# Attention and routed experts: the block of values one chunk later, the load of V in its own pair

## The chip, the cores and the metric

The kernel runs on one core of a Trainium2 chip. The metric is the device time of one execution in microseconds: the median of several runs, lower is better. Engines are called PE or TensorE (matmul; PEld is its weight load), ACT or ScalarE, DVE or VectorE, POOL or GpSimd, and SP, which here only issues DMAs.

## The reference

Attention for 8 batches of 8 heads, 576 positions, 64 features, with a decaying bias from a running sum, is followed by a layer of 8 experts of which each of the 4608 tokens takes one:

```python
scores = scale * np.matmul(q, k.transpose(0, 1, 3, 2))
cum = np.cumsum(np.maximum(s, 0.0), axis=-1)
bias = -(cum[:, :, :, None] - cum[:, :, None, :])
scores = np.where(causal, -1000000000.0, scores + np.minimum(bias, 0.0))
scores = scores - np.max(scores, axis=-1, keepdims=True)
attn = np.exp(scores)
attn = attn / (np.sum(attn, axis=-1, keepdims=True) + 1e-09)
x = np.matmul(attn, v)            # then heads side by side: 4608 x 512
...
e_idx = np.argmax(x @ w_gate + modality_bias[modality_id], axis=1)
...
h = np.maximum(x[mask] @ w1[e], 0.0)
out[mask] = gate_w[mask, None] * (h @ w2[e])
```

## The kernel before

**Two stages.** The attention stage takes some 380 us of the span, the expert stage the rest. The expert stage begins when attention's last rows have been written, gathered and turned.

**Pairs and chunks.** The 64 (batch, head) combinations are worked as 32 pairs: two batches of one head. The rows of scores of a pair are cut into nine chunks: 0 to 3 are the four blocks of 128 rows of the first batch, 4 to 7 those of the second, 8 is the last 64 rows of both together. The mask is causal, so chunk `c` or `4 + c` is 128 x 128(c + 1), and chunk 8 is 128 x 576. `ORDER = (3, 7, 2, 6, 8, 1, 5, 0, 4)` is the order in a pair, the wide ones first.

**One loop of steps.** `run` (L500) has one step for each chunk, nine a pair; `k % 9` is the step in the pair. A step does, in the order of the text:

- `score` (L375): the scores of this chunk by matmuls on PE (L372 and L394; L407 and L408 for chunk 8) into a PSUM buffer `sp` (four buffers); the bias, the mask and the row minimum of the negated scores on DVE (L396, L410); the exponential on ACT (L416).
- sometimes a piece of set-up, a load (`load_v`, L307, in step 5; `load_qk`, L300, in step 7), and a piece of `prep` (L312) for the next pair: copies to KB by DMA (L332), splitting of Q and K into high and low parts on POOL (L322, L326).
- a piece of `tail` (L455) of the pair before, if one is open.
- `trans` (L418) for the chunk of three steps ago (`LAG = 3`): transposes on PE (L433, L448) into a PSUM buffer `pt` (two buffers), copied to PT in SBUF by ACT (L437) or, for chunk 8, by DVE (L451, L453). Chunks 0 and 4, and chunks 1 and 5, share one buffer and one copy (`JOINT`): nothing is done at the first of the two. The transposes of the last chunk of a pair thus come in step 2 of the next pair, and with them the tail of the pair is opened.
- pieces of routing work (`bg`), in steps 0, 1 and 5 (`QUIET`) or in each step.

**The tail.** It is a generator, one piece a step. It first yields `TD` times, then does the block of values (L474): 36 matmuls that multiply PT by V into PSUM `o` and one buffer of `sp`, and the copies to `oT` on ACT (L477) and DVE (L480). The next piece makes the reciprocal row sums `rs` (L484, L485) and the first products of `oT` with the gate weights (L346, `pw` and `pq`, into PSUM `ox`, taken to `x` by DVE, L495 and L497), the piece behind it the second products. With `TD = 1` the block is in step 4.

**What sets the order.** A planner puts the instructions of each engine in order by a model of its own; where two are ready it goes by the text. It may move work, but not past explicit orders: the block stands behind every matmul and transpose of PE recorded since the last block (`self.pe`), and everything of attention that PE gets after it in the text stands behind the block (`wall`, through `behind`). So the block is a fence on PE. Each engine then takes its work in that order; DMAs of SP are issued one after the other.

**V.** `V` has two buffers. The first two loads are made before the loop. In step 5 of pair `pi` the load for pair `pi + 1` follows; it takes the buffer that the block of pair `pi - 1`, one step earlier, has read. `start` takes the tile out of `self.V` when the pair begins.

Of the kernel before, what the change touches and what calls it, by code (L numbers as in the profile page):

```python
# [23 lines left out]
EXT = 76  # L24
ORDER = (3, 7, 2, 6, 8, 1, 5, 0, 4)
LAG = 3
TD = 1
SPB = 4
PTDVE = (8,)
JOINT = (0, 1)  # L30
# [8 lines left out]
class Attn:  # L39
# [318 lines left out]
        return after  # L358

    def start(self, pi, x):  # L360
        st = dict(pi=pi, h=pi % 8, x=x, s={}, high={}, PT=self.PT[pi % 2], V=self.V.pop(pi))
        st["mx"] = self.sm.tile([P, 10], F32, name="mx")
        st["sums"] = self.sm.tile([P, 9], F32, name="sums")
        return st
# [90 lines left out]
    def tail(self, st):  # L455

        nc = self.nc
        V, PT, x, h = st["V"], st["PT"], st["x"], st["h"]
        for _ in range(TD):
            yield  # L460
# [39 lines left out]
    def run(self, npair, newx, done, setup):  # L500

        bg = self.bg = []
        seq = [(pi, i) for pi in range(npair) for i in ORDER]
        sts = {}
        prev, prepg, n = [], None, len(seq)
        for k in range(n + LAG + 9):
            if k < n:
                pi, i = seq[k]
                if k % 9 == 0:
                    sts[pi] = self.start(pi, newx(pi // 8) if pi % 8 == 0 else sts[pi - 1]["x"])  # L510
                    prepg = self.prep(pi + 1) if pi + 1 < npair else None
                with self.behind() if pi or not self.pe else self.tc.issue_after(self.pe[-1]):
                    self.score(sts[pi], i)
                if k in setup:
                    with self.newest():
                        more = setup[k]()
                        if more is not None:
                            bg.append([more, False])
                if k % 9 == 5 and 0 < pi < npair - 1:
                    self.V[pi + 1] = self.load_v(pi + 1)  # L520
                if k % 9 == 7 and 0 < pi < npair - 2:
                    self.raw[pi + 2] = self.load_qk(pi + 2)
                if prepg is not None:
                    next(prepg, 0)
            if prev and next(prev[0][0], 0) == 0:
                _, st = prev.pop(0)
                if st["pi"] % 8 == 7:
                    bg.append([done(st["pi"] // 8, st["x"]), False])
            for j in () if k == LAG else (0, 1) if k == LAG + 1 else (k - LAG,) if LAG < k < n + LAG else ():
                p0, i0 = seq[j]  # L530
                with self.behind():
                    self.trans(sts[p0], i0)
                if i0 == ORDER[-1]:
                    prev.append((self.tail(sts[p0]), sts[p0]))
            if not prev and k >= n + LAG:
                break
            for b in list(bg):
                if k >= b[1] if b[1] > 1 else k % 9 in QUIET or not b[1]:
                    with self.newest():
                        b[1] = next(b[0], None)  # L540
                    if b[1] is None:
                        bg.remove(b)
        assert not prev
        return bg
# [847 lines left out]
```

## Time and profile before

| | us |
|---|---|
| median of 3 runs | 834.55 |
| lowest, highest | 834.48, 834.68 |
| profiled execution: its own time | 833.09 |
| profiled execution: span of the trace | 831.3 |
| block of values, start to start, in most pairs | 10.8 to 11.4 |
| the block itself, modelled ends | 2.96 |

The span runs from the first to the last instruction of the trace; the execution's own time includes what lies around it. The granted clock of TensorE is 0.996 of full over the span and 1.00 in the attention stage after the start. A row of the timeline gives start, length, engine, line of the kernel, operation and operands, `xN` for N like ones in a row, and in brackets the idle time of the engine before it and what ended it.

### The profile page before, as it was taken

How to read it: one execution, taken by the hardware profiler on the slowest of the kernel's cores; microseconds unless marked ns; L12 is line 12 of the kernel's file. 1: busy time of each engine (PE TensorE's matmuls, PEld its weight loads, DVE VectorE, ACT ScalarE, POOL GpSimd, SP SyncE). 2: the span in 40 equal slices, each digit the busy share in tenths (PEclk: the TensorE clock that was granted, in tenths of full speed). 3: DMA queues.
4: the chain of work that ended last, by engine and by line, in shares of the span. 5: the costliest groups of instructions: out<-in, count | busy, mean ns of one | idle time of the engine just before them, and what ended most of it. 6: DMA issues, size and time to landing. Idle time of an engine off the chain costs nothing. (4 is left out here: it accounts for less than half of the span.)

```text
span 831.3 us, 17195 instructions
## 1 busy us (share of the span) xinstructions
PE 807.9 (97%) x5948; PEld 696.2 (84%) x5948; DVE 526.3 (63%) x1405; ACT 524.6 (63%) x1164; POOL 360.8 (43%) x383
## 2 busy tenths in 40 slices
PE   7999999999999999998999999999999999999996
PEld 6777778887787788877888999998888999988884
DVE  7555566655666666756479865565666655555865
ACT  6767778877887878875365554454455554444653
POOL 8768778888789877993501000000000000000002
PEclk9999999999999999999999999999999999999999
DMA  7575466676557655558597866565556776555960
GB/s 235 156 222 173 139 213 192 211 233 205 162 175 229 204 180 178 183 182 292 202 394 292 312 257 256 200 223 204 208 203 245 257 257 245 203 206 207 376 235 29
DMA packets 68551, 182.35 MB, mean 219 GB/s; under 512 B 7993, under 2 KB 8889, under 8 KB 68334
## 3 DMA queue, kind: packets, MB, share of 16 engines
q1 hardware_dynamic: 62622, 161.17, 57.7%
q0 software_dynamic: 5840, 20.06, 6.2%
q8 instruction: 48, 0.79, 0.4%
q14 instruction: 41, 0.34, 0.1%
HBM read 144.73 MB, written 26.80 MB: 206 GB/s over the span
## 5 line engine op out<-in xcount | busy, mean ns | idle before, releaser
L1073 POOL DMA_INDIRECT out<-ys,oi x36 | 37.1, 1031 | 370.2 <-ACT ys L1072 298.9
L416 ACT ACTIVATE pe<-pe,mx 128x512 f32<-128x512 f32 (+3 forms) x256 | 142.6, 559 | 12.1 <-DVE mx L396 11.5
L396 DVE CUSTOM_DVE_ANT_0 pe<-sp,mk 128x512 f32<-128x512 f32 (+3 forms) x256 | 117.8, 485 | 48.2 <-PE sp L394 22.7
L437 ACT COPY PT<-pt 128x512 f32<-128x512 f32 (+1 forms) x192 | 94.1, 505 | 41.8 <-PE pt L433 41.7
L433 PE MATMUL pt<-ident,pe 128*128 128x128 f32 x640 | 109.2, 277 | 3.6 <-ACT pe L416 2.9
L372 PE MATMUL sp<-KA,QH 128*128 128x256 f32 (+2 forms) x256 | 98.9, 393 | 3.5 <-POOL KA L236 2.5
L1089 ACT ACTIVATE hT<-hp 128x512 fp32r<-128x512 f32 x72 | 42.9, 596 | 92.8 <-PE hp L1087 92.3
L474 PE MATMUL o<-PT,V 128*64 128x256 f32 (+3 forms) x512 | 87.2, 440 | 4.4 <-ACT PT L437 4.3
L1087 PE MATMUL hp<-xT,wcb 128*128 128x256 f32 x648 | 89.6, 282 | 0.0
L1087 PE MATMUL hp<-xT,wca 128*128 128x256 f32 x624 | 87.3, 282 | 0.5 <-ACT xT L1039 0.5
L433 PEld LDWEIGHTS pt<-ident,pe 128*128 128x128 f32 x640 | 76.6, 143 | 13.3 <-ACT pe L416 8.3
L326 POOL TENSOR_TENSOR QL<-rawq,QH 64x576 fp32r<-64x576 f32 x62 | 86.7, 1415 | 0.1
L326 POOL TENSOR_TENSOR KA<-rawk,KA 64x576 fp32r<-64x576 f32 x62 | 86.6, 1414 | 0.3
L394 PE MATMUL sp<-KB,QL 76*128 76x256 f32 (+2 forms) x256 | 84.4, 337 | 0.5 <-DMA KB<-KA 0.4
L1087 PEld LDWEIGHTS hp<-xT,wcb 128*128 128x128 f32 x648 | 83.1, 188 | 0.6
L1090 DVE SCALAR_TENSOR_TENSOR hT<-hp,hT 128x512 fp32r<-128x512 f32 x72 | 49.5, 688 | 53.0 <-ACT hT L1089 52.9
L1087 PEld LDWEIGHTS hp<-xT,wca 128*128 128x128 f32 x624 | 80.5, 188 | 1.4 <-issue 0.7
L1062 PE MATMUL y<-wcb,hT 128*128 128x512 f32 x336 | 81.2, 398 | 0.0
L1062 PEld LDWEIGHTS y<-wcb,hT 128*128 128x128 f32 x336 | 62.8, 188 | 14.7
L474 PEld LDWEIGHTS sp<-PT,V 128*64 128x64 f32 x640 | 39.4, 137 | 34.4 <-issue 22.0
L322 POOL TENSOR_SCALAR KA<-rawk 128x576 fp32r<-128x576 f32 x60 | 39.8, 672 | 58.8 <-PE sp L372 35.3
L1087 PE MATMUL hp<-xT,wcc 128*128 128x256 f32 x456 | 64.6, 281 | 0.0
(287 smaller groups left out, 1679.6 us busy)
## 6 DMA issues: line engine op xcount, KB each, us to landing
wrbw<-in_w SPq DMA_DIRECT2D x104, 512.0 KB
wraw<-in_w SPq DMA_DIRECT2D x56, 512.0 KB
rawq<-in_qkv SPq DMA_DIRECT2D x31, 576.0 KB
rawk<-in_qkv SPq DMA_DIRECT2D x31, 576.0 KB
xg<-lists SPq DMA_DIRECT2D x18, 576.0 KB
V<-in_qkv SPq DMA_DIRECT2D x32, 320.0 KB
KB<-KA SPq DMA_DIRECT2D x62, 144.0 KB
lists<-z SPq DMA_DIRECT2D x8, 576.0 KB
```

Source lines behind the costliest of these rows:

```text
L326: self.last = nc.gpsimd.tensor_tensor(o, i, h, ALU.subtract).ins
L372: self.pe.append(self.nc.tensor.matmul(sp[:, :nn], QH[:, q0:q0 + P], self.KA[u][:, ab, :nn], start=True, stop=False).ins)
L394: self.pe.append(nc.tensor.matmul(sp[:, :nn], QL[:EXT, q0:q0 + P], KB[:EXT, ab, :nn], start=False, stop=True).ins)
L396: ins = nc.vector.tensor_tensor_reduce(out=t[:, :n], in0=sp[:, :n], in1=self.mk[:, 512 - n:512], scale=-0.125, scalar=3.0e38, op0=ALU.add, ...
L416: self.act = nc.scalar.activation(t[:, :n], t[:, :n], AF.Exp, bias=m, scale=-1.0, accum_out=st["sums"][:, o:o + 1]).ins
L433: self.pe.append(nc.tensor.transpose(out=pt[:, o:o + P], in_=pe[:, P * j:P * j + P], identity=self.ident).ins)
L437: cp(w[:, :, :, v:v + P], pt[:, :n * (1 + both)].rearrange("p (a j q) -> p a j q", a=1 + both, q=P))
L474: m = nc.tensor.matmul(t[r, q0 - b:q1 - b], V[:, ab, j, :], PT[:, ab, PTS * j + q0 if j < 4 else PTW - 64:PTS * j + q1 if j < 4 else PTW], ...
L1062: self.last[0] = nc.tensor.matmul(y[u], hT[:, a, f, P * u:P * u + P], W[4 + f // 2][:, c, 512 * (f % 2):512 * (f % 2) + 512], start=f == 0 ...
L1087: nc.tensor.matmul(hp[:, u], W[k][:, a, f:f + P], xT[:, c, k], start=k == 0 and i == 0, stop=k == 3 and i == 2)
L1089: hi = nc.scalar.activation(hs, hp, AF.Relu)
L1090: lo = nc.vector.scalar_tensor_tensor(hT[:, 1, 2 * m:2 * m + 2], hp, 0.0, hs.bitcast(F32), ALU.max, ALU.subtract)
```

## The change

`TD` becomes 2, so the tail of a pair waits one more step before the block of values: it stands in step 5 instead of step 4, and all the pieces of the tail behind it are one step later too. Since the block of pair `pi - 1` is now in step 5 of pair `pi`, after the place of the old load in the text, the load is moved: the load of pair `pi`'s own V is issued in step 2 of pair `pi`, for all pairs from 2 on. `start` accepts that V is not there yet.

```diff
-TD = 1
+TD = 2
...
-        st = dict(pi=pi, h=pi % 8, x=x, s={}, high={}, PT=self.PT[pi % 2], V=self.V.pop(pi))
+        st = dict(pi=pi, h=pi % 8, x=x, s={}, high={}, PT=self.PT[pi % 2], V=self.V.pop(pi, None))
...
-                if k % 9 == 5 and 0 < pi < npair - 1:
-                    self.V[pi + 1] = self.load_v(pi + 1)
+                if k % 9 == 2 and pi > 1:
+                    sts[pi]["V"] = self.load_v(pi)
```

## The prediction, made before the changed kernel was run

> **What bounds the kernel now.** I read the page first, then a table of windows cut from one block of values (L474) to the next, then the list of waits, then the timeline around two blocks.
>
> ```profile
> span 831.3 us, 17195 instructions
> PE 807.9 (97%) x5948; PEld 696.2 (84%) x5948; DVE 526.3 (63%) x1405; ACT 524.6 (63%) x1164; POOL 360.8 (43%) x383
> ```
>
> TensorE has no room: 97% of the span is matmul. What can be gained lies in its gaps. In the table of windows each row is one pair of the attention stage, from the start of its block to the start of the next (length, then busy time of each engine):
>
> ```profile
> 176.76:188.12 11.36, 11.04 (x95) 9.08 (x95) 6.76 (x29) 8.75 (x27) 9.46 (x11) 1.00 0.68 218
> ...
> 211.12:221.92 10.80, 10.80 (x97) 9.08 (x96) 7.00 (x32) 8.80 (x28) 7.28 (x8) 1.00 0.59 174
> ...
> 233.11:243.92 10.81, 10.81 (x97) 9.08 (x96) 7.24 (x32) 9.18 (x28) 7.75 (x9) 1.00 0.59 173
> ```
>
> The same work takes 11.36 us in one pair and 10.80 in another, at the same granted clock of 1.00: 0.56 us of the long one is no work. PE's busy time shows only 11.36 - 11.04 = 0.32 of it. The list of waits has the rest; its columns are total us, times, longest:
>
> ```profile
> PEld o L474 <- ACT PT L437: 8.0, 15, 0.7
> PEld pt L433 <- ACT pe L416: 7.7, 22, 1.3
> ```
>
> Fifteen blocks wait 8.0 us together, 0.53 us each, for a copy of PT on ScalarE, which is nearly what a long pair has over a short one. The second row, transposes that wait for an exponential, I leave as it is: the change keeps the distance from a score to its transposes.
>
> [...] The same list has this wait once more, as the matmuls show it:
>
> ```profile
> PE o L474 <- ACT PT L437: 4.3, 14, 0.5
> ```
>
> By the matmuls' row the full stake would be 4.3 us, by the loads' row 8.0. [...]
>
> Why the copy is late is seen in the timeline before the block at 188.12 (start, length, engine, line):
>
> ```profile
> 184.76 0.59 ACT L437 COPY PT<-pt 128x512 f32<-128x512 f32 x1 [1.23 <-PE pt L433]
> ...
> 185.69 0.73 ACT L416 ACTIVATE pe<-pe,mx 128x512 f32<-128x512 f32 x1
> ...
> 186.41 0.71 ACT L416 ACTIVATE pe<-pe,mx 128x512 f32<-128x512 f32 x1
> ...
> 187.12 0.60 ACT L416 ACTIVATE pe<-pe,mx 128x384 f32<-128x384 f32 x1
> ...
> 187.51 0.29 PE L408 MATMUL sp<-KB,QL 76*128 76x288 f32 x1
> ...
> 187.72 0.35 ACT L437 COPY PT<-pt 128x256 f32<-128x256 f32 x1
> ...
> 188.12 0.20 PEld L474 LDWEIGHTS o<-PT,V 128*64 128x64 f32 x4 [0.55 <-ACT PT L437]
> ```
>
> ScalarE does the three widest exponentials of the next pair (chunks 3, 7, 2) before the small copy of 256 columns that completes PT. It ends at 188.07; TensorE's scores of chunk 8 began their last matmul at 187.51 and nothing else was allowed before the block.
>
> **The change part by part.** *TD from 1 to 2.* The transposes of chunk 7 (step 4) and the score of chunk 1 (step 5) now come ahead of the block; they used to be the first thing behind it. The timeline of TensorE after the block that ends at 202.4 prices them by start to start:
>
> ```profile
> 202.36 0.66 PE L433 MATMUL pt<-ident,pe 128*128 128x128 f32 x4
> 202.77 0.36 PE L372 MATMUL sp<-KA,QH 128*128 128x256 f32 x1
> ...
> 203.09 0.66 PE L346 MATMUL ox<-pw,oT 128*128 128x144 f32 x4
> ...
> 203.76 0.49 PE L433 MATMUL pt<-ident,pe 128*128 128x128 f32 x3
> 204.00 0.36 PE L372 MATMUL sp<-KA,QH 128*128 128x256 f32 x1
> ...
> 204.33 0.49 PE L433 MATMUL pt<-ident,pe 128*128 128x128 f32 x3
> ...
> 205.87 0.40 PE L372 MATMUL sp<-KA,QH 128*128 128x512 f32 x1
> ...
> 206.34 0.65 PE L346 MATMUL ox<-pw,oT 128*128 128x144 f32 x4
> ```
>
> Transposes of 7: 202.77 - 202.36 = 0.41. Score of 1: 203.09 - 202.77 = 0.32. Together 0.73 us of work for a wait of 0.53, so at first sight all of it is covered. But PSUM's `pt` has two buffers taken in turn (chunks 3, 7, 2, 6, 8, the joint 1 and 5, the joint 0 and 4: seven a pair, so 7 takes the one that the joint 0 and 4 held). The transposes of 7 therefore cannot start before the very copy that the block waited for. Only the score of 1 covers, if the planner puts it first: 0.32 of 0.53. Ends: nothing gained (transposes first, same wait under another name), 8.0 us gained. I take the score's cover: **15 x 0.32 = 4.8 us**.
>
> *What is late next.* Behind the block the first products with the gate weights (L346) need oT, which is copied out when the block ends. The same stretch on the other engines:
>
> ```profile
> 202.30 0.59 ACT L477 COPY oT<-o 128x512 f32<-128x512 f32 x1 [1.03 <-PE o L474]
> ...
> 202.48 0.46 DVE L480 COPY oT<-sp 64x64 f32<-64x64 f32 x2 [2.76 <-PE sp L474]
> ...
> 202.98 0.55 PEld L346 LDWEIGHTS ox<-pw,oT 128*128 128x128 f32 x4
> ```
>
> oT is complete at 202.94 and its first weight load starts at 202.98: just in time. The cover was 0.73 us (7 and 1); in the new order it is the three transposes of chunk 2 (204.00 - 203.76 = 0.24) and the score of chunk 5 (204.33 - 204.00 = 0.33), 0.57 us. The load could then start 0.16 earlier, at 202.82, and would wait 0.12 us. Over 31 pairs that is 3.7 us if TensorE keeps this order, and nothing if the transposes of 6 go first. The planner does move what is not ready: the second group of these products (206.34 above) belongs to the step of chunk 5's score by the text and runs behind the next pair's first score (205.87). So I take the middle, **1.9 us lost**.
>
> *The queue of ScalarE.* The copy of oT now has the copy of 7 and the exponential of 1 ahead of it. By form, over the attention stage (count, busy us, mean ns, idle us before):
>
> ```profile
> L416 ACT ACTIVATION_READ_ACCUMULATOR pe<-pe,mx 128x1 f32 x245 | 46.3, 189 | 0.0
> ...
> L416 ACT ACTIVATE pe<-pe,mx 128x256 f32<-128x256 f32 x62 | 31.7, 511 | 5.8 <-DVE mx L396 5.8
> ...
> L477 ACT COPY oT<-o 128x512 f32<-128x512 f32 x32 | 18.8, 586 | 29.0 <-PE o L474 29.0
> ```
>
> The copy of 7 takes 0.59 (as at 184.76) and the exponential 0.51 with some 0.09 of its readout behind it: 1.19 us more. ScalarE idles 29.0 / 32 = 0.91 us before the copy of oT, and the block ends 0.73 later, so 1.64 us are there: 0.45 to spare. Cost nothing in the mean; below it is a rival, since the idle time differs from pair to pair.
>
> *The load of V.* It is issued by SP in step 2 of its own pair, not in step 5 of the pair before. SP around it, then what the page says of sizes and of the load on the queues:
>
> ```profile
> 195.83 0.47 SPq L332 DMA_DIRECT2D KB<-KA  x1
> 200.65 0.36 SPq L304 DMA_DIRECT2D rawq<-in_qkv  x1
> 203.38 0.36 SPq L304 DMA_DIRECT2D rawk<-in_qkv  x1
> 203.83 0.38 SPq L309 DMA_DIRECT2D V<-in_qkv  x1
> ```
>
> ```profile
> DMA packets 68551, 182.35 MB, mean 219 GB/s; under 512 B 7993, under 2 KB 8889, under 8 KB 68334
> ...
> rawq<-in_qkv SPq DMA_DIRECT2D x31, 576.0 KB
> ...
> V<-in_qkv SPq DMA_DIRECT2D x32, 320.0 KB
> ```
>
> Before, V left at 203.83 for the block at 221.92, 18 us ahead; its buffer was in use until 202.4, so it could not leave sooner. Now its buffer has been free since the block before, and the load follows the copies to KB into a stretch in which SP issues nothing (196.30 to 200.65). A load that leaves at 196.3 serves the block at 211.12, which will stand at about 211.9: 15 us ahead. Its 320 KB are 1.5 us at the page's mean of 219 GB/s, and with two pieces of 576 KB before it 6.7 us (an estimate from these rows). It is late only if loading takes twice that; the price would be a wait at the block, where the list has none on a DMA. Behind it on SP stand rawq and rawk, which it delays by its issue, 0.38 us, and by its 1.5 us of traffic; rawk no longer has V between it and the next copies to KB. Nothing is gained by that, since SP's idle stretch of 4.3 us lies in between. I take nothing either way.
>
> *The rest.* `start` only allows a missing V. The routing of a group begins one step later and meets the same steps 0, 1 and 5 for most of its pieces: nothing. The expert stage starts on attention's last output, so the gain carries over:
>
> ```profile
> 384.07 6.30 PE L1087 MATMUL hp<-xT,wca 128*128 128x256 f32 x48 [0.45 <-ACT xT L1039]
> ```
>
> **Sum.** -4.8 + 1.9 = -2.9 us. The profiled execution took 833.09 us (1.8 outside its span), which gives 830.2; the median of the runs shown is 834.55, 1.46 above it, which gives **831.6 us**.
>
> **The rivals.**
>
> *A, the whole wait goes.* The exponentials of 3, 7 and 2 begin earlier, because less of ScalarE's work lies between the block's end and them (copy of 7 and exponential of 1 are done), and the copy is early as in the pair of 10.80. For it: that pair exists, with the same work. Against: in the long pair ScalarE waits 1.23 us at 184.76 for TensorE, so its load there was not the limit. 834.55 - 8.0 = 826.6.
>
> *B, the wait only changes its name.* The transposes of 7 go first and wait for the same copy through `pt`; then the score, then the block. For it: that is the order of the text. Against: the planner puts ready work first. Gain 0, less up to 1.9: 834.5 to 836.5, say 835.
>
> *C, slower: the copy of oT is late on ScalarE.* The rows before 188.12 show ScalarE taking its work one piece after the other, the small copy behind three large exponentials. Where the idle time before that copy is short, the 1.19 us do not fit. One pair as it stands:
>
> ```profile
> 358.29 0.59 ACT L477 COPY oT<-o 128x512 f32<-128x512 f32 x1 [0.28 <-PE o L474]
> ```
>
> Here 0.28 + 0.73 - 1.19 = -0.18: the copy, and the products behind it, would be 0.18 us late. It is worse where the exponentials run closer together, which is what a shorter pair does. At 0.30 us late in each of 31 pairs the loss is 9.3, less the 4.8 gained: 834.55 + 4.5 = 839.0. From 4.8 / 31 = 0.15 us late per pair on, the change loses. Against it: the mean has 0.45 to spare.
>
> [...]
>
> *D, nothing of it shows:* the block keeps its place. The order behind all earlier scores and transposes is written out, so I give it little: 834.5.
>
> **How the numbers follow.** Forecast 38% (829.7 to 833.5, the two middle terms at their ends), A 20%, B 20%, C 20%, D 2%. Some 0.2%, 1.7 us, is about what a measurement can tell from no change, so faster means under 832.9 and slower over 836.2. Of the forecast three quarters are faster: 28 + 20 = 48, say 49%. Same: 10 + 15 of B + 2, 27%. Slower: C and the rest of B, 24%. The range reaches from A with another microsecond of waits gone (825.5) to C (839.0).
>
> **What would show it.** Right: the wait of `o L474` on PT falls from 8.0 us to near 0, a wait of `pt L433` on ACT PT of some 3 us appears, long pairs come to about 11.1 us. A: the long pairs are 10.8. B: that new wait is near 8 us. C: a wait of `ox L346` on ACT oT of 5 us or more, and pairs that were 10.8 are longer. It would be wrong altogether if the planner, given the new order, moves other work of the pair: the exponentials' place against the small copy decides between 10.8 and 11.36 now, and no row shows how it will fall.

## The result and the profile after

| | before | after |
|---|---|---|
| median, us | 834.51 (4 runs, 834.41 to 834.68) | 840.11 (4 runs, 838.37 to 840.92) |
| ratio after / before | | 1.0064, 95% interval 1.0047 to 1.0081 |
| span of the profiled execution | 831.3 | 838.1 |
| start of the 2nd block of values | 38.66 | 42.85 |
| start of the 32nd (last) block | 376.90 | 384.69 |
| first matmul of the experts (L1087) | 384.07 | 391.87 |

The changed kernel is 5.6 us slower, where 2.9 us faster was forecast, and it lies above C's 839.0, the upper end of the forecast's range. The table says where: 4.2 us are lost before the second block, 3.6 more up to the last block, and the expert stage of this execution is 1 us shorter (from its first matmul to the end 447.2 us before, 446.2 after). So there are two losses, in two places. Two single executions in the experiments below, one of e9 (2017 us) and one of e10 (1313 us), took far longer than the others of their kernel and are left out of the ratios, though not of the medians. The page after has TensorE as full as before:

```profile
span 838.1 us, 17128 instructions
...
PE 813.7 (97%) x5948; PEld 696.9 (83%) x5948; DVE 531.6 (63%) x1405; ACT 527.3 (63%) x1164; POOL 360.6 (43%) x383
```

97% again, though 6.8 us are lost: PE's busy time rose by 5.8 us for the same 5948 matmuls. The share of busy time does not show this loss.

**The first loss, at the start.** The table of windows cut from block to block (length, busy time of each engine with its instructions, granted clock, DMA share, GB/s), first pair before:

```profile
27.25:38.66 11.41, 11.07 (x97) 9.04 (x96) 7.90 (x38) 9.15 (x30) 6.67 (x19) 1.00 0.70 226
```

The same of the kernel after: the first pair, then a long and a short pair of the middle of the stage:

```profile
27.89:42.85 14.96, 12.92 (x96) 10.46 (x96) 8.44 (x37) 8.58 (x28) 12.04 (x29) 0.89 0.64 189
193.78:205.25 11.47, 11.12 (x96) 9.01 (x96) 6.84 (x28) 8.90 (x27) 9.06 (x10) 1.00 0.66 212
239.52:250.53 11.01, 10.99 (x96) 8.99 (x95) 6.99 (x33) 8.94 (x30) 7.77 (x9) 1.00 0.58 169
```

The first pair takes 14.96 us instead of 11.41, and POOL has 29 instructions in it, not 19. The timeline behind the first block after says what they are (start, length, engine, line):

```profile
31.90 0.23 ACT L609 CAST tok<-ti 128x36 f32<-128x36 int32 x1 [2.34 <-POOL ti L608]
...
32.11 0.20 ACT L612 CAST e<-ei 128x8 f32<-128x8 int32 x1
32.21 0.58 ACT L477 COPY oT<-o 128x512 f32<-128x512 f32 x1
32.34 1.15 DVE L614 TENSOR_SCALAR ecap<-e 128x8 f32<-128x8 f32 x1 [3.96 <-ACT e L612]
...
32.93 0.73 PE L346 MATMUL ox<-pw,oT 128*128 128x144 f32 x4 [1.38 <-ACT oT L477]
...
33.47 0.45 DVE L480 COPY oT<-sp 64x64 f32<-64x64 f32 x2
```

L609, L612 and L614 are the routing's constants: lists of numbers that POOL writes (L606, L608, L611) and ScalarE and VectorE convert, once in a run. They are made in step 5 of pair 1, where the block of pair 0 now stands. By the text they come right ahead of it, so ScalarE waits 2.34 us for POOL, VectorE 3.96 us for ScalarE, and the copies of oT stand behind both. TensorE idles 1.38 us, and the next pair starts late.

The clock has a part in it. The 0.89 of this window is one stretch of 3.41 us, from 34.37 to 37.78, at a granted clock of 0.50. Of the 3.55 us that the first pair is longer, 1.85 are longer matmuls (12.92 against 11.07 busy), and half of 3.41, some 1.7 us, is an estimate of what the low clock cost; the rest is idle time. The kernel before has such a stretch too, but at 11.69 to 15.10, ahead of its first block. In e9 below, which has the same collision, it comes at 34.78 to 38.19, again right behind the idle time. That the idle time brings it about is not shown: no run changes one without the other.

**The second loss, in every pair.** From the 4th block to the 31st are 27 pairs: before from 64.06 to 367.44, 11.236 us each; after from 68.06 to 375.58, 11.390 each. That is 0.154 a pair, 4.2 us. The long pairs went from 11.36 to 11.47, the short ones from 10.80 to 11.01. The waits of the weight loads in the attention stage after (total us, times, longest) against those quoted in the prediction:

```profile
PEld ox L346 <- DVE xq L497: 9.7, 31, 0.9
PEld pt L433 <- ACT PT L437: 7.9, 14, 0.7
PEld pt L433 <- ACT pe L416: 7.6, 21, 1.3
...
PEld o L474 <- ACT PT L437: 0.7, 1, 0.7
```

The block's wait for PT fell from 8.0 us to 0.7, and the same 8 us stand one line up, as transposes that wait for the same copy. The row on top is new but for one time of 0.9 us: the second products with the gate weights wait for VectorE in each pair. A wait that each pair had before, chunk 8's transposes for ScalarE's copies (`PEld pt L448 <- ACT PT L437`, 5.3 us, 31 times), is not in the list after. The end of a long pair after shows the first of the two:

```profile
203.78 0.29 PE L408 MATMUL sp<-KB,QL 76*128 76x288 f32 x1
...
204.02 0.28 PE L394 MATMUL sp<-KB,QL 76*128 76x256 f32 x1
...
204.26 0.35 ACT L437 COPY PT<-pt 128x256 f32<-128x256 f32 x1
...
204.66 0.66 PE L433 MATMUL pt<-ident,pe 128*128 128x128 f32 x4 [0.35 <-ACT PT L437]
...
205.25 0.65 PE L474 MATMUL o<-PT,V 128*64 128x512 f32 x2
```

The planner did put the score of chunk 1 (204.02) ahead of the transposes of chunk 7 (204.66), as the prediction had it. Yet the copy of 256 columns ends at 204.61, 0.83 us after the last matmul of chunk 8's scores began (203.78). In the pair of the prediction it was 188.07 - 187.51 = 0.56. The copy came 0.27 us later, nearly all of the 0.32 that the score covers, and the transposes wait for it in the block's stead. It is so in the other long pairs too (0.54 to 0.56 before, 0.82 or more after); why the copy is later stays open.

The second products after, with VectorE's last read of `ox`, their weight loads and their neighbours on PE:

```profile
199.73 0.28 DVE L497 TENSOR_SCALAR xq<-ox,rs 128x72 f32<-128x72 f32 x1
199.85 0.27 PE L433 MATMUL pt<-ident,pe 128*128 128x128 f32 x1
...
200.07 0.54 PEld L346 LDWEIGHTS ox<-pw,oT 128*128 128x128 f32 x4 [0.31 <-DVE xq L497]
200.07 0.76 PE L346 MATMUL ox<-pw,oT 128*128 128x144 f32 x4
...
200.66 0.49 PE L433 MATMUL pt<-ident,pe 128*128 128x128 f32 x3
...
200.91 0.48 PE L372 MATMUL sp<-KA,QH 128*128 128x512 f32 x1
```

They stand inside a group of four transposes and take 200.66 - 200.07 = 0.59 us from start to start. Before, the pair in the prediction has them between a score and transposes, at 206.34; what follows there starts 0.49 later:

```profile
206.11 0.67 PEld L346 LDWEIGHTS ox<-pw,oT 128*128 128x128 f32 x4
...
206.83 0.38 PE L433 MATMUL pt<-ident,pe 128*128 128x128 f32 x2
```

Two things differ: the neighbours, and the first weight load. Before, the load starts 0.23 us ahead of its matmul. After, it starts with it, because VectorE empties `ox` only at 199.73 + 0.28 = 200.01. The same rows over the 27 pairs, in four kernels, tell the two apart (mean us from the start of the products to the start of what follows):

| what follows | load starts ahead of its matmul | load starts with its matmul |
|---|---|---|
| transposes | 0.49 (before, 21 pairs) | 0.59 (after, 27 pairs) |
| a score | 0.40 (e11, 27 pairs) | 0.50 (e5, 16 pairs) |

A late load adds 0.10 in both rows. What stands ahead made no difference here: the products are inside transposes in 3 pairs before and in 26 after, and those 3 take 0.49 like the rest. The 0.09 between the rows of the table is not saved: a score of 512 columns took 0.32 to 0.33 us to its second matmul behind transposes or products, and 0.23 behind another score (medians, before and e11). The late load also holds its own matmul back: from the transpose ahead of it 0.21 after, 0.11 in the 3 pairs before. So **the wait for VectorE costs 0.09 + 0.10 = 0.20 us a pair** (0.198 before rounding), 5.3 us in the 27.

The first products went from 0.667 to 0.724, 1.5 us. It is the same thing in small: their first load starts 0.05 us behind the end of ScalarE's copy of oT in every pair, and 0.05 ahead of its matmul, where it was 0.12 before. No list of waits has it, since the load before it runs until then. Together 6.8 us, which is more than the 4.2 of the second loss: the pairs' other time got shorter, by 2.6.

### The profile page after: what moved, and what is told of

Same layout as the page of the kernel before. It is cut to its first block, busy times and chain, and to the rows that moved or that the text cites. A ratio compares the mean times of both kernels' runs of the same rounds, so it can differ in the third digit from the quotient of the medians.

```text
span 838.1 us, 17128 instructions
## 1 busy us (share of the span) xinstructions
PE 813.7 (97%) x5948; PEld 696.9 (83%) x5948; DVE 531.6 (63%) x1405; ACT 527.3 (63%) x1164; POOL 360.6 (43%) x383
## 5 line engine op out<-in xcount | busy, mean ns | idle before, releaser
L396 DVE CUSTOM_DVE_ANT_0 pe<-sp,mk 128x512 f32<-128x512 f32 (+3 forms) x256 | 117.7, 487 | 51.6 <-PE sp L394 28.4
L437 ACT COPY PT<-pt 128x512 f32<-128x512 f32 (+1 forms) x192 | 96.2, 502 | 48.2 <-PE pt L433 46.4
L433 PE MATMUL pt<-ident,pe 128*128 128x128 f32 x640 | 115.6, 280 | 9.0 <-ACT PT L437 5.6
L372 PE MATMUL sp<-KA,QH 128*128 128x256 f32 (+2 forms) x256 | 96.8, 385 | 2.1 <-POOL KA L236 1.8
L433 PEld LDWEIGHTS pt<-ident,pe 128*128 128x128 f32 x640 | 74.8, 143 | 24.4 <-ACT PT L437 8.9
L1087 PE MATMUL hp<-xT,wcb 128*128 128x256 f32 x648 | 89.6, 282 | 0.0
L1087 PE MATMUL hp<-xT,wca 128*128 128x256 f32 x624 | 87.3, 282 | 0.5 <-ACT xT L1039 0.4
L326 POOL TENSOR_TENSOR QL<-rawq,QH 64x576 fp32r<-64x576 f32 x62 | 87.2, 1422 | 0.1
L326 POOL TENSOR_TENSOR KA<-rawk,KA 64x576 fp32r<-64x576 f32 x62 | 86.7, 1414 | 0.2
L1087 PEld LDWEIGHTS hp<-xT,wcb 128*128 128x128 f32 x648 | 83.1, 188 | 0.6
L394 PE MATMUL sp<-KB,QL 76*128 76x256 f32 (+2 forms) x256 | 82.5, 329 | 0.4 <-DMA QL<-ek 0.4
L1087 PEld LDWEIGHTS hp<-xT,wca 128*128 128x128 f32 x624 | 80.5, 188 | 1.4 <-issue 0.7
L480 DVE COPY oT<-sp 64x64 f32<-64x64 f32 x64 | 14.2, 222 | 79.5 <-PE sp L474 79.1
```

Of the source, the lines that this page charges most:

```text
L326: self.last = nc.gpsimd.tensor_tensor(o, i, h, ALU.subtract).ins
L372: self.pe.append(self.nc.tensor.matmul(sp[:, :nn], QH[:, q0:q0 + P], self.KA[u][:, ab, :nn], start=True, stop=False).ins)
L394: self.pe.append(nc.tensor.matmul(sp[:, :nn], QL[:EXT, q0:q0 + P], KB[:EXT, ab, :nn], start=False, stop=True).ins)
L396: ins = nc.vector.tensor_tensor_reduce(out=t[:, :n], in0=sp[:, :n], in1=self.mk[:, 512 - n:512], scale=-0.125, scalar=3.0e38, op0=ALU.add, ...
L433: self.pe.append(nc.tensor.transpose(out=pt[:, o:o + P], in_=pe[:, P * j:P * j + P], identity=self.ident).ins)
L437: cp(w[:, :, :, v:v + P], pt[:, :n * (1 + both)].rearrange("p (a j q) -> p a j q", a=1 + both, q=P))
```

## The experiments

Ratios are to the kernel before, run on the same chip, with 95% intervals; "mean pair" is that of the 27 pairs, as above.

| | median us | ratio | span | mean pair |
|---|---|---|---|---|
| after | 840.11 | 1.0064 (1.0047 to 1.0081) | 838.1 | 11.390 |
| e1: after, constants in step 6 | 836.28 | 1.0042 (1.0026 to 1.0059) | 834.4 | 11.390 |
| e2: before, constants in step 4 | 835.38 | 1.0029 (1.0013 to 1.0044) | 833.1 | 11.321 |
| e3: before, load of V moved | 832.94 | 1.0001 (0.9982 to 1.0021) | 831.5 | 11.263 |
| e4: e1, row sums early | 828.83 | 0.9951 (0.9934 to 0.9968) | 827.0 | 11.121 |
| e5: before, row sums early | 828.91 | 0.9941 (0.9923 to 0.9959) | 828.0 | 11.096 |
| e6: before, joint copy on VectorE | 828.82 | 0.9938 (0.9920 to 0.9957) | 828.8 | 11.063 |
| e7: e4 and joint copy on VectorE | 827.14 | 0.9918 (0.9897 to 0.9939) | 825.3 | 10.980 |
| e8: e5 and joint copy on VectorE | 825.66 | 0.9902 (0.9871 to 0.9934) | 824.1 | 10.894 |
| e9: after, row sums early | 830.46 | 0.9946 (0.9928 to 0.9964) | 830.4 | 11.129 |
| e10: e1 and joint copy on VectorE | 830.54 | 0.9960 (0.9945 to 0.9975) | 828.0 | 11.104 |
| e11: e4, second products a step later | 817.02 | 0.9787 (0.9771 to 0.9803) | 815.9 | 10.752 |
| e12: e11 and joint copy on VectorE | 817.62 | 0.9803 (0.9786 to 0.9819) | 815.8 | 10.734 |
| e13: e5, second products in step 8 | 822.33 | 0.9861 (0.9833 to 0.9889) | 818.8 | 10.847 |
| e14: e5, second products in step 7 | 826.24 | 0.9895 (0.9876 to 0.9915) | 826.1 | 10.964 |

The kernel before had medians of 832.96 beside e1 to e4, 833.68 beside e5 to e7, 834.00 beside e8 to e10, 834.35 beside e11 and e12 and 834.45 beside e13 and e14, so medians of different groups are compared by their ratios. A single pair can differ by almost 1 us between two executions (the 30th takes 11.98 us before and 12.84 in e3), so 0.03 in the mean pair tells nothing.

**The start: e1 and e2.** e1 moves the constants behind the block; e2 gives the kernel before the same collision, since its block is in step 4.

```diff
 # e1, in the kernel after
-            setup = {..., 14: R.consts, ...}
+            setup = {..., 15: R.consts, ...}
 # e2, in the kernel before
-            setup = {..., 14: R.consts, ...}
+            setup = {..., 13: R.consts, ...}
```

> The changed kernel with the set-up of the routing constants one step later (step index 15, not 14). Theory 1: at 14 these constants stand, in the text, just ahead of the first block of values, and the copies of its result to oT queue behind them on ScalarE and VectorE; the second block then starts 4.2 us later than in the kernel before. Moved, that loss goes: 840.1 - 4.2 = 835.9, within 0.8, and the wait of 1.4 us of ox L346 on ACT oT is gone. Rival, the load of V disturbs SP's queue: no change, 840. Rival, the copy of oT is late in every pair: no change, 840.

Measured: the second block at 39.04 instead of 42.85, 3.8 us earlier, and the span 3.7 shorter; the pairs are as in the kernel after, 11.390. The window of the first pair and the timeline behind the first block in e1:

```profile
28.33:39.04 10.71, 10.71 (x97) 9.06 (x96) 6.81 (x35) 8.34 (x26) 9.53 (x27) 1.00 0.60 201
```

```profile
31.11 0.59 ACT L477 COPY oT<-o 128x512 f32<-128x512 f32 x1 [1.09 <-PE o L474]
...
33.13 0.21 ACT L609 CAST tok<-ti 128x36 f32<-128x36 int32 x1
```

The copy of oT (31.11) now runs ahead of the conversions (33.13), and the clock of this pair is 1.00, with 27 instructions of POOL in it. By the same estimate some 1.7 of the 3.8 us are the low clock, of which e1's trace has nothing in the attention stage. By the medians, each against its own kernel before, the loss went from 5.6 to 3.3 us, near what the second loss leaves; by the ratios it fell by 1.8 us only, and the intervals overlap, so the size stands on the trace.

> The kernel before with the same constants one step earlier (13, not 14), so that they stand just ahead of its own first block. Theory 1: the same collision in the kernel without the change, 834.5 + 3 to 4.5 = 837.5 to 839. Both rivals: the constants have nothing to do with it, 834.5.

Measured: the first pair takes 12.89 us instead of 11.41, 1.5 more, and the ratio gives 2.4 us. The 32nd block starts 2.2 us later (379.14 against 376.90), but that holds single pairs that differ by up to 1 us either way (the third 12.32 against 13.35, the 30th 13.07 against 11.98). The timeline of e2 has the same picture as the kernel after:

```profile
30.07 0.23 ACT L609 CAST tok<-ti 128x36 f32<-128x36 int32 x1 [1.34 <-POOL ti L608]
...
30.38 0.58 ACT L477 COPY oT<-o 128x512 f32<-128x512 f32 x1
...
31.10 0.48 PE L346 MATMUL ox<-pw,oT 128*128 128x144 f32 x2 [0.56 <-ACT oT L477]
```

The direction is right, the size smaller than expected: POOL is done sooner here, ScalarE waits 1.34 us and not 2.34, TensorE 0.56 and not 1.38, and the clock of this pair is 1.00. What follows: the first loss is this collision, with the low clock that came with it in the kernel after, and it can be had without the block's later place.

**The load of V: e3.**

```diff
 # in the kernel before, TD = 1
-                if k % 9 == 5 and 0 < pi < npair - 1:
-                    self.V[pi + 1] = self.load_v(pi + 1)
+                if k % 9 == 2 and pi > 1:
+                    sts[pi]["V"] = self.load_v(pi)
```

> The kernel before with the load of V alone moved as in the change; the block stays one step after the tail is opened. Theory 1: the load does not matter, 834.5 within 0.7. Rival, the load of V disturbs SP's queue: most of the loss is here, 838 to 840.

Measured: ratio 1.0001, and its interval leaves no room for a cost above 1.8 us. As expected against its own kernel before, the move costs nothing that is seen. (e3 has the changed `start` too.) In the kernel after SP has the load still behind rawk and as soon as the block has freed the buffer (the block ends at 208.21):

```profile
208.27 0.36 SPq L304 DMA_DIRECT2D rawk<-in_qkv  x1
208.72 0.38 SPq L309 DMA_DIRECT2D V<-in_qkv  x1
```

**The row sums: e4, e5, e9.** The reciprocal row sums `rs` are made in the block's step, not one step later. They need only the sums of the exponentials, which are there by then. It was meant to free VectorE sooner, since the second products wait for the first ones' buffer, which VectorE empties with `rs`.

```diff
             nc.vector.tensor_copy(oT[r, 512 + 64 * ab:576 + 64 * ab], ox[r, :64])
-        yield
         rs = self.sm.tile([P, 9], F32, name="rs")
         with self.tc.issue_after(self.hold[0]), self.tc.issue_after(self.act):
             nc.scalar.activation(rs, st["sums"], AF.Identity, bias=self.eps[:, :1])
             nc.vector.reciprocal(rs, rs)
+        yield
```

> The changed kernel with the constants later (as in the first run) and with the reciprocal row sums made in the step of the block, no longer one step behind it. Theory 1: the second loss is that the second products with the gate weights wait for VectorE to empty ox (L497), 9.7 us by the weight loads, 0.31 us in each of 31 pairs, because the reciprocals come late. Made early, that wait falls below 2 us and the time to 835.9 less 31 x 0.15 to 0.25, 828 to 831.5; pairs that took 11.0 to 11.1 us are back at 10.8. If that wait costs nothing, because TensorE would have waited for something else: 835.5 to 836.5. Rival, the copy of oT late on ScalarE: 836 or more, with waits of ox L346 on ACT oT.

> The kernel before with the reciprocal row sums made in the step of the block. Theory 1 (they cost only where they are late: in the kernel before, the second products do not wait for ox in steady state): no change against the kernel before, within 1.0 us, long pairs still 11.3 to 11.4. Rival (the early reciprocals are a gain by themselves, and the block one step later brought nothing to the 4.1 us by which the corrected version beat the kernel before): 4 us faster, long pairs 11.1.

e4 came out in the expected time, with the long pairs at 11.13; the short ones are 10.91, not 10.8. e5 fell against the theory on record: it expected no change and the kernel before gains as much, 0.9941. So the early sums are a gain of their own, with the block in either place. VectorE is done with `ox` (end of L497) 5.04 us behind the start of the block in e4 and 6.21 in e1, 5.15 in e5 and 6.51 before, in the mean of the 27 pairs. One row of VectorE's waits before looks like the cause and is not:

```profile
DVE pe L396 <- ACT rs L484: 22.0, 24, 0.9
```

In each of these 24 waits the row of scores gets its own matmuls only after 0.8 us, and ScalarE's part of `rs` comes 0.11 us behind them: 2.7 of the 22.0 us. Where the rest of e5's gain lies stays open, since the second products do not come late in the kernel before.

The waits of the weight loads in e4:

```profile
PEld pt L433 <- ACT pe L416: 10.1, 39, 0.7
PEld pt L433 <- ACT PT L437: 2.9, 14, 0.2
...
PEld ox L346 <- DVE xq L497: 0.9, 1, 0.9
```

The wait of 9.7 us of the second products is gone from the list, and so is the 0.057 us by which the first products had grown (0.667 again; ScalarE's copy of oT ends 0.055 us sooner behind the start of the block). But the second products still take 0.594 us, as in e1. In all 27 pairs their first load still waits for VectorE, 0.09 us, which is too short for the list, and still starts with its matmul; only the time ahead of it fell, from 0.21 to 0.12.

> The changed kernel with the reciprocals early and the constants left where they were. Theory 1, two losses that add: slower than the corrected version by the start alone, 3 to 4.2 us, so about 832.5 against a kernel before of 833, with the second block near 43 us and long pairs of 11.13. If the two act on each other: long pairs other than 11.13, or a second block before 41.

e9 leaves the constants where they collide. Its mean pair is 11.129 and its last block starts at 376.41, 3.2 us behind that of e4 (373.20), with the second block at 42.54: in this execution the two losses add, as expected. The times do not bear it out. The ratio, 0.9946, is that of e4, where 3 to 4.2 us more were expected, and the profiled execution took 832.46 us where the eight others behind the ratio took 830.2 to 830.6. So it is not shown that the loss at the start comes in each execution of e9.

**The joint copy: e6, e7, e8, e10.** The copy of 256 columns goes to VectorE, so that no exponential stands ahead of it.

```diff
-PTDVE = (8,)
+PTDVE = (8, 4)
```

> The kernel before with the joint copy of the transposes of chunks 0 and 4 on VectorE in place of ScalarE. Theory 1: that copy stands behind three exponentials and is what the block waits for (8.0 us, 15 times). On VectorE it is early, the wait on ACT PT goes to below 1 us; the copy delays the reductions by some 0.35 us a pair, part of which comes back as a wait of transposes for exponentials: 2 to 6 us faster than the kernel before. Rival (the block would have waited anyway, since scores and exponentials end there too): no change within 1 us, with a new wait of 7 us or more at the block or at the transposes.

> The changed kernel with the constants later and the joint copy on VectorE, the reciprocals where the change puts them. If the wait of the transposes of chunk 7 is for the joint copy through the buffer pt (rival B of the prediction), the 7.9 us of pt L433 on ACT PT fall below 1.5 us and long pairs from 11.47 to the 11.0 to 11.1 of the short ones: 5 to 7 us faster than the run with the constants later alone, ratio to the kernel before 0.995 to 0.999. If that wait is for something else: long pairs stay at 11.3 or more.

> The corrected version (block one step later, constants later, reciprocals early) with the joint copy on VectorE. Theory 1: the rest of the wait through pt (2.9 us by the weight loads) goes, long pairs fall from 11.13 to about 10.95: 2 to 4 us faster than the corrected version, 5 to 8 faster than the kernel before. Rival: VectorE's queue takes the gain back, no change against the corrected version.

> The kernel before with the two gains that need no change of the block's place: reciprocals early and the joint copy on VectorE. If the block's later place is worth nothing (reciprocals early gave long pairs of 11.10 us without it and 11.13 with it), this is at least as fast as the corrected version with the joint copy (ratio 0.9918): long pairs 10.8 to 10.95, ratio 0.988 to 0.992. If the later place is worth something once the other waits are gone: long pairs 11.0 or more, ratio 0.993 or more.

In the kernel before (e6) this takes 0.62% off the time, 5.2 us, near the 4.8 that the prediction hoped to win from this wait. The long pairs fall from 11.36 to 10.97, 0.39 us for a wait of 0.53 each by the loads' row and 0.31 by the matmuls'. In the kernel after with its constants moved (e10) the long pairs fall from 11.46 to 10.90, the rows of waits on ScalarE's PT are gone, and this one stays:

```profile
PEld ox L346 <- DVE xq L497: 10.0, 32, 0.9
```

So the new wait of the transposes was the old one, for the same copy, through the two buffers of `pt`: rival B. e7 is 2.8 us faster than e4 by the ratios and 1.7 by the spans, where 2 to 4 were expected. e8 has the same two edits with the block in its old place and is not slower than e7.

**The place of the second products: e11 to e14.** One more piece of the tail, ahead of the second products. In e13, with the block in its old place, two pieces, so that these products stand in step 8 as in e11; in e14 one.

```diff
         for g in (1, 0):
+            if not g:
+                yield
             for u in range(2):
```

> The corrected version (block one step later, constants later, reciprocals early) with the second products with the gate weights one step later in the text, so that the planner puts them between two scores and no longer inside a group of transposes. Theory 2: in the changed kernel these four matmuls take 0.56 us from start to start in the mean, 0.45 in the kernel before, because they interrupt a group of transposes in 26 of 27 pairs (3 of 27 before); between two scores the kernel before has them at 0.40. So 0.16 us less in each pair: pairs of 11.13 and 10.91 become 10.97 and 10.75, 4 to 5 us faster than the corrected version, ratio to the kernel before 0.989 to 0.991. Rival (their place does not matter, TensorE is held by ScalarE's copies): pairs unchanged, ratio 0.995.

> The same with the joint copy on VectorE. Theory 2: pairs of 10.92 become 10.75, ratio to the kernel before 0.986 to 0.989, the fastest of all: then the block one step later does pay, once the three things that the change brought or left are dealt with. Rival (place does not matter): ratio 0.992, as without the step.

e11 gained more than twice what was expected: 0.9787, 817.0 us, and 11.1 us in the spans against e4, where 4 to 5 were expected. Its windows (an ordinary pair and one with a piece of routing) and its rows on PE around the second products:

```profile
192.76:203.46 10.70, 10.70 (x97) 9.04 (x96) 7.48 (x31) 9.00 (x26) 10.48 (x11) 1.00 0.60 203
214.15:225.20 11.05, 11.05 (x106) 9.38 (x105) 8.04 (x36) 9.42 (x29) 8.54 (x9) 1.00 0.58 170
```

```profile
198.18 0.56 PEld L346 LDWEIGHTS ox<-pw,oT 128*128 128x128 f32 x4
198.18 0.28 PE L394 MATMUL sp<-KB,QL 76*128 76x256 f32 x1
...
198.30 0.66 PE L346 MATMUL ox<-pw,oT 128*128 128x144 f32 x4
...
198.70 0.49 PE L372 MATMUL sp<-KA,QH 128*128 128x512 f32 x1
...
199.26 0.60 PE L433 MATMUL pt<-ident,pe 128*128 128x128 f32 x4
...
199.61 0.48 PE L372 MATMUL sp<-KA,QH 128*128 128x512 f32 x1
```

They now stand between two scores in all 27 pairs and take 198.70 - 198.30 = 0.40 us. The four transposes of one chunk are together again: 199.61 - 199.26 = 0.35 us. In the kernel after the same two things took 200.91 - 199.85 = 1.06 us, here 0.75. The neighbours are not the reason, as theory 2 had it. VectorE is done with `ox` 5.04 us behind the start of the block, as in e4, and the products now start 5.54 behind it and not 5.09, so their first load (198.18) is 0.12 us ahead of its matmul again. That is worth 0.10 against e4, by the table of the second loss; the 0.09 that a score behind them seems to save comes back in that score. Another part shows on VectorE: the first wide row of scores (L396, 128x512) starts 6.77 us behind the start of the block, 7.30 in e4. The exponentials behind it follow earlier, and the waits of TensorE for them shrink, in e11:

```profile
PEld pt L433 <- ACT pe L416: 2.5, 7, 0.6
```

10.1 us in e4, 2.5 here; in the 27 pairs 6.5 and 0.3, which is 0.23 a pair. With the 0.10 of the loads that makes 0.33 of the gain of 0.37 us a pair, an estimate from the waits; no run has one part without the other. e12 was expected to be the fastest and is level with e11, as the intervals overlap: but for one time, no wait for the joint copy was left to take away.

> The block in its old place (one step after the tail is opened), reciprocals early, and the second products with the gate weights in step 8, where the fastest run with the moved block has them: the two differ in the block's place alone. If the later block pays once its costs are off: long pairs still wait for the joint copy (0.24 us or more at the block), 10.9 to 11.1, ratio to the kernel before 0.985 to 0.99. If the block's place is worth nothing and the gain was all in the place of the second products: all pairs 10.7, ratio 0.977 to 0.981.

> The same with the second products in step 7, one step behind their old place (the same single step that was added to the version with the moved block); the planner then puts them between a score and the transposes of chunk 8. If what counts is that they do not stand inside transposes and free VectorE before the scores of 4 and 3: 10.75 to 10.9, ratio 0.98 to 0.985. If only the place between two scores counts: 11.0 to 11.1 as with early reciprocals alone, ratio 0.994.

These two separate the block's place from the place of the products. e14 lies between e5 and e13, and its ratio, 0.9895, between what its two theories expected. e13 has the early sums, its second products mostly between scores and the constants behind the block, like e11, but the block in step 4. Its ratio is in the range for a block whose later place pays, though its long pairs, at 10.80, are below it. There the wait of the block itself stays:

```profile
PEld o L474 <- ACT PT L437: 5.5, 18, 0.7
```

Its mean pair is 10.847 against 10.752 in e11: 0.095 × 27 = 2.6 us for the block's later place, 2.9 in the spans (818.8 against 815.9) and 6.2 by the ratios of the medians (the profiled execution of e13 was its fastest, that of e11 its slowest). **So the later place is a gain once its costs are off**, about as large as what the prediction had forecast for the whole change. The wait that the prediction looked at is only part of it. In the traces 2.0 of the 2.6 us lie in the first eight of the 27 pairs, where e13's weight loads wait 1.5 us for POOL's part of K (`KA`, L326) and e11's never; in the other 19 it is 0.03 a pair, though e13's block waits 0.27 in most long pairs there. The fastest versions are e11, 2.1% under the kernel before, and e12, both with the changed kernel's `TD = 2`.

## Why the prediction was wrong

- **"*The rest.* ... nothing": wrong, +3.8 us.** It weighed the routing that runs all along and not the set-up of step 5 of pair 1, which the block was moved behind. The conversions ahead of the copies of oT on ScalarE and VectorE were in `run`'s list of set-up pieces and could have been read there. e1 and e2 show the collision; some 1.7 of the 3.8 us are the half-clock stretch, which the prediction had no term for.
- **"Only the score of 1 covers ... 15 x 0.32 = 4.8 us": the term that failed in the pairs.** The score came first, as assumed, but the wait was as long behind it, 7.9 us in 14 transposes instead of 8.0 in 15. The term held the copy's end fixed against the scores of chunk 8, and it came 0.27 us later. This is rival B, and e10 shows that it is the same copy. Its price was given as 0 to 1.9 us lost and the pairs lost 4.2, so B is right in its mechanism and not in its sum.
- **"the middle, 1.9 us lost" for the first products: right in mechanism, the size by luck.** The load does wait for oT in every pair, as the prediction's order of transposes and score had it. It costs 0.057 us in each, half of the 0.12 that was read, 1.5 us in 27 pairs. The 1.9 came out near it because 3.7 was halved for another reason, that the planner might keep this order or not.
- **The second products were counted at nothing.** The prediction used them as proof that the planner moves what is not ready, and did not ask whether `ox` would be empty in the place where they would be put. The planner put them 6.27 us behind the start of the block, where VectorE is done with `ox` at 6.21, and 0.20 × 27 = 5.3 us are lost on a weight load that comes too late. It is the case that its last paragraph named, the planner moving other work of the pair; what decided was these products, not the exponentials. The cause is read from the rows of four kernels; e4 and e11, which shorten this wait and take it away, are both faster, but both change more than that.
- **"*The queue of ScalarE* ... Cost nothing in the mean": held.** ScalarE still idles before the copy of oT (17.6 us in 31 pairs by its waits, 0.57 each, against 0.91 before), and the copy starts 2.83 us behind the start of the block in both kernels. So rival C, a copy of oT that is late in ScalarE's queue, is not seen in the pairs; the first products wait for it because less stands ahead of them. C's time, 839.0, was near the result for another reason.
- **"*The load of V* ... I take nothing either way": right in cost, wrong in place.** The load did not go into SP's idle stretch; the planner issues it as soon as the buffer is free, as before (208.72, above). e3 shows the cost: none.
- **The sum's own idea holds in part.** In the changed kernel it brought nothing of the 4.8: the wait of 8 us stayed. With the costs off, the block's later place is worth 2.6 us in the pairs and 2.9 in the spans (e11 against e13). That this is near the forecast's 2.9 is luck, since most of it is not the wait for the copy of PT.

## What to carry to other kernels

When a fence is moved by a step, list everything that the text issues in the step it is moved to, in the first pairs too: work done once can stand ahead of it in each engine's queue, as the routing's constants did here (3.8 us). A wait that goes says little until the copy behind it is followed to its next reader; here, with the copy on VectorE, the long pairs got shorter with the fence in either place, by 0.39 us in e6 and 0.56 in e10. Price the work that the planner pushes aside by its start-to-start time in its new place, and look whether its first weight load starts ahead of its matmul there: neither the share of busy time (97% before and after) nor the list of waits (9.7 us in 31, 0.31 each) gave the 0.20 us a pair that the late load cost here. Compare rows that share their neighbours before the neighbours are called the cause.

## What the runs showed of the hardware

- **A weight load that started with its matmul and not ahead of it lengthened the group by 0.10 us.** The same four matmuls (L346, 128x144) took 0.49 us to the transposes behind them with the load 0.11 us or more ahead (before) and 0.59 with it late (after and e4); to a score behind them 0.40 (e11) and 0.50 (16 pairs of e5), at a granted clock of 1.00. Transposes or a score ahead of them made no difference (0.49 in both, before).
- **Neither busy share has this loss.** The matmuls are at 97% before and after and the loads at 84% and 83%, with 696.2 and 696.9 us; the start of single loads and the time from one block to the next decided. For the block's wait on PT, 0.53 us each by the loads' row and 0.31 by the matmuls', e6 measured 0.39 us a long pair, between the two.
- **ScalarE and VectorE did not pass a waiting instruction.** In the first pair ScalarE stood 2.34 us and VectorE 3.96 before conversions that e1 makes later at no cost that is seen, with copies behind them that TensorE waited for.
